# Two query tiles' scores in one TensorE visit, transpose mode for batch 0, and 128-row last stores that end on 16 outer steps

## The chip, the cores and the metric

The kernel runs on one core of a Trainium2 chip. The metric is the device time of one execution in microseconds, taken as the median of several runs. The engines are TensorE (PE; its weight loads are listed as PEld), VectorE (DVE), ScalarE (ACT), GpSimd (POOL) and SyncE (SP), which issues most DMAs.

## The reference

Eight batches of eight heads; 512 local and 32 global tokens per head, head size 64. A local query sees the 32 global keys and the local keys at most 32 places away; a global query sees all. The 4608 x 512 result goes through a layer with a Mish activation. The weights arrive as 64-bit floats.

```python
def _attn_ref(q_l, k_l, v_l, q_g, k_g, v_g):
    k_all = np.concatenate([k_g, k_l], axis=2)
    v_all = np.concatenate([v_g, v_l], axis=2)
    s_g = scale * np.matmul(q_g, k_all.transpose(0, 1, 3, 2))
    out_g = np.matmul(sm(s_g), v_all)                       # sm: softmax over the last axis
    s_ll = scale * np.matmul(q_l, k_l.transpose(0, 1, 3, 2))
    s_ll = np.where(np.abs(pos[:, None] - pos[None, :]) <= 32, s_ll, -1000000000.0)
    s_lg = scale * np.matmul(q_l, k_g.transpose(0, 1, 3, 2))
    a_l = sm(np.concatenate([s_lg, s_ll], axis=-1))
    out_l = np.matmul(a_l, np.concatenate([v_g, v_l], axis=2))
    return np.concatenate([out_g, out_l], axis=2)

def _moe_ref(x, w_in, w_out):                               # x: 4608 x 512, d_ff 2048
    h = x @ w_in
    g = h * np.tanh(np.log1p(np.exp(h)))                    # for h <= 20
    return g @ w_out
```

## The kernel before

Two heads share the 128 partitions, so a batch has four head pairs (`hp`). The 512 local queries of a pair are four tiles `t` of 128; a tile sees a window of 192 or 224 keys, global ones included (`WIN`: 192, 224, 224, 192). For each unit (batch, pair, tile) the work is a chain over the engines:

- `scores` (L611): two fp32 products on TensorE, one per head, each with K = 64 on its own half of the array's rows, into two buffers `s` of the PSUM ring "sc" (three buffers, shared with `g` and `gu` of the global queries);
- `row_max` (L620, VectorE) adds the mask and takes the row's extreme while it copies the scores to `P`; `expo` (L629, ScalarE) takes the exponential and the sums;
- `P` is split into two fp16 parts `ph` and turned by a transposing DMA into `pt` (`p_hi`, `p_lo`, `p_turn`); in batch 0 (`TURNED = 1`) TensorE turns `P` instead by products with the identity (`p_cross`, L667, into `PT`), and likewise the normalised result `x` (`x_cross`, L682, into `XT`);
- `pv` (L702): 12 small fp16 products of `pt` with the values, into `U`; then normalisation and a second turn into `xh` and `xl`, the layer's inputs.

Once per head pair the 32 global queries go through the same steps on a path of their own: `g_scores` (L740, fp32, two halves of 64 columns of the array), and `g_pv` (L794), whose result goes to `xg`.

The layer works on 17 blocks of 256 rows: 16 of local rows, the last (block 16) of all the global rows in `xg`. Each block has 8 steps: `m1_mm` (L838, fp16 products into `h`), `mish` (L881, ScalarE), `g_hi` and `g_lo` (VectorE mostly, into `G`), `m2_mm` (L906, into `o`). `store` scales `o` into `ob` and sends it out. Each product is made of three fp16 products (high by high, high by low, low by high).

At the start, the 64-bit weights are loaded on ScalarE's DMA queue, rebuilt as fp32 by VectorE (L418 to L427), measured by TensorE (`w_stat`, L439) and split into two fp16 parts (`w_split`, with `rest` on TensorE for the first layer, L483).

The order on each engine is not the order of the code. A planner (`Plan`) gets every piece of work with its engine, an assumed duration and what it reads and writes, and lists it: of the pieces that are ready, the one with the lowest number goes first on its engine. The numbers follow the order in which `slot(u)` adds the work for unit `u`. Engines then run their lists in that order, with semaphores between them. In the last store of block 16, ScalarE scales the first 128 rows and VectorE the second, and SP issues both transfers; their target is written as 4 batches x 32 rows x 512 floats.

Of the kernel before, what the change touches and what calls it, by code (L numbers as in the profile page):

```python
# [240 lines left out]
def attn_mish_kernel(ctx: ExitStack, tc: tile.TileContext, qt, kt, vm, vg, qg, w1, w2, consts_in, out, w64):  # L241
# [76 lines left out]
    def dma(kib):  # L318
        return kib * 2.81
# [282 lines left out]


    def scores(b, hp, t):
        q, k, s = ("q", b, hp), ("k", b, hp), [("s", b, hp, t, h) for h in range(2)]
        c0, w, m0 = WIN[t]

        def go():
            for h in range(2):
                r = slice(h * 64, h * 64 + 64)  # L610
                T.matmul(X[s[h]][:, :w], X[q][r, t * 128:(t + 1) * 128], X[k][r, c0:c0 + w], start=True, stop=True)  # L611
        pl.add(PE, 620, go, r=[q, k], new=[("sc", s[0]), ("sc", s[1])], rows=0.5)

    def half(P, h, w):
        return X[P][:, h * 224:h * 224 + w]

    def row_max(b, hp, t, h):
        s, P, nm = ("s", b, hp, t, h), ("P", b, hp, t), ("nm", b, hp, t, h)
        c0, w, m0 = WIN[t]
        pl.add(DVE, 155 + 1.04 * w, lambda: V.tensor_tensor_reduce(  # L620
            out=half(P, h, w), in0=X[s][:, :w], in1=mask[:, m0:m0 + w], scale=-SCALE, scalar=3.0e38, op0=ALU.add, op1=ALU.min,
            accum_out=X[nm]), r=[s, "consts"], w=[[P, h]] if h else (), new=[("nm", nm)] if h else [("P", P), ("nm", nm)])

    def expo(b, hp, t, h):
# [33 lines left out]
    def p_cross(b, hp, t):  # L658

        P, pt, PT = ("P", b, hp, t), ("pt", b, hp, t), ("PT", b, hp, t)  # L660
        rows = 128 if t else 96

        def go():
            for h in range(2):
                for c in range(2):
                    c0, n = h * 224 + c * rows, h * 2 + c
                    T.matmul(X[PT][:rows, n * 128:(n + 1) * 128], X[P][:, c0:c0 + rows], ident, start=True, stop=True)  # L667
        pl.add(PE, 1000, go, r=[P, "consts"], new=[("h", PT)], rows=0.5)

        def part(p):  # L670
            return X[pt][:rows, p * 4:p * 4 + 4, :].rearrange("p n q -> p (n q)")
        pl.add([(ACT, act(512)), (DVE, dve(512))], 0, lambda e: scaled(e, part(0), X[PT][:rows], PSC), r=[PT], new=[("pt", pt)])
        pl.add(DVE, dve(512), lambda: V.scalar_tensor_tensor(part(1), X[PT][:rows], PSC, part(0), ALU.mult, ALU.subtract), r=[PT], w=[pt])

    def x_cross(b, hp, t):
        g, ts = group(b, hp, t)
        x, XT, n, c0 = ("x", *g), ("XT", *g), 128 * len(ts), ts[0] * 128
        first = hp == 0 and ts[0] == 0

        def go():  # L680
            for i, u in enumerate(ts):
                T.matmul(X[XT][:, i * 128:(i + 1) * 128], X[x][:, u].rearrange("p h d -> p (h d)"), ident, start=True, stop=True)  # L682
        pl.add(PE, 250 * len(ts), go, r=[x, "consts"], new=[("h", XT)], rows=0.5)
        hi, lo = ("xh", b), ("xl", b)
        keys = [(hp, h) for h in range(2) if 2 * h in ts]
        cut = lambda name: X[name][:, hp, c0:c0 + n]
        pl.add([(ACT, act(n)), (DVE, dve(n))], 0, lambda e: copy(e, cut(hi), X[XT][:, :n]), r=[XT], w=[[hi, k] for k in keys],
               new=[("xh", hi)] if first else ())
        pl.add(DVE, dve(n), lambda: V.tensor_tensor(cut(lo), X[XT][:, :n], cut(hi), ALU.subtract), r=[XT] + [[hi, k] for k in keys],
               w=[[lo, k] for k in keys], new=[("xl", lo)] if first else ())  # L690
# [94 lines left out]
    def g_pv(b, hp):  # L785
# [11 lines left out]
        pl.add(PE, mm(18, 69), go, r=[pt, vf, va], new=[("sc", u)])  # L797
        for h in range(2):
            r = slice(64 * h, 64 * h + 64)
            pl.add([(ACT, 290), (DVE, 158)], 0, lambda e, r=r, h=h: scaled(e, xg[r, hp, b * SG:(b + 1) * SG], X[u][r, 32 * h:32 * h + 32],  # L800
                                                                          X["sv", b][r, 2:3]), r=[u, ("sv", b)], w=[["xg", (b, hp, h)]])


# [109 lines left out]
    def store(blk):  # L913
        ob = ("ob", blk)
        for t in range(2):
            o, c = ("o", blk, t), ("c", blk)
            engs = [(ACT, 690), (DVE, 668)] if blk < 2 * B else [((ACT, 690), (DVE, 668))[t]] * 2
            pl.add(engs, 0, lambda e, t=t, o=o: scaled(e, X[ob][:, t], X[o], X[c][:, 1:2]), r=[o, [c, 1]], w=[[ob, t]],
                   new=() if t else [("ob", ob)])
            if blk < 2 * B:  # L920
                r0 = (blk // 2) * S + SG + (blk % 2) * TB + t * 128
                pl.add(DMA, dma(256), lambda r0=r0, t=t: load(out[r0:r0 + 128, :], X[ob][:, t]), r=[[ob, t]])
            else:
                a = out[t * 4 * S:(t * 4 + 1) * S, :]
                pl.add(DMA, dma(256), lambda a=a, t=t: load(bass.AP(a.tensor, a.offset, [[S * DM, 4], [DM, SG], [1, DM]]), X[ob][:, t]),
                       r=[[ob, t]])


    NU = B * 16
# [21 lines left out]
    def slot(u):  # L951
# [14 lines left out]
        for x in m:  # L966
            if x[1] == 0:
                blk_start(x[0])
        if fu:
            scores(*fu)  # L970
        if fu:
            row_max(*fu, 0)
# [213 lines left out]
```

## Time and profile before

| | |
|---|---|
| median of 3 runs | 994.0 us (993.28 to 994.28) |
| the profiled execution | 989.48 us, of which the span from the first to the last instruction is 987.5 us |
| mean granted TensorE clock | 0.988 |
| busy: PE, PEld, DVE, ACT, POOL | 946.3, 633.0, 568.0, 583.1, 12.8 us |
| DMA | 113.73 MB in 214392 packets |

A line of the timeline gives a start, a duration, engine, source line, operation, output and inputs, shapes and a count of merged instructions; in square brackets stands how long the engine was idle before and what released it. `L12` is line 12 of the kernel. A matmul's recorded duration includes its way through the array, so neighbouring matmuls overlap in time; what one costs in a stream is the distance between starts.

### The profile page before, as it was taken

The numbers are of one execution on the slowest core, as the hardware profiler recorded it, in microseconds if no ns is written. First come the engines' busy times: TensorE is split into PE (matmuls) and PEld (weight loads), VectorE is DVE, ScalarE is ACT, GpSimd is POOL, SyncE is SP. The second block draws the span as 40 slices with busy tenths as digits, with TensorE's granted clock in tenths as the row PEclk, the third lists the DMA queues.
The fourth block names the chain that finished last, engine by engine and source line by source line (L and its number), as shares of the span: only waits on it lengthen the run. The fifth ranks groups of instructions, "written<-read, shape, count | busy, mean of one in ns | idle before, by whom it ended". The sixth has DMA issues, their size and how long they took to land.

```text
span 987.5 us, 20674 instructions
## 1 busy us (share of the span) xinstructions
PE 946.3 (96%) x8124; PEld 633.0 (64%) x8124; DVE 568.0 (58%) x1733; ACT 583.1 (59%) x1187; POOL 12.8 (1%) x25
## 2 busy tenths in 40 slices
PE   4789899999999999999999999999999999999995
PEld 2556677666675666666666666666666666666663
DVE  6879777747777665755465556665555542322221
ACT  2356876767676686768676777586676751211110
POOL 3000000000000000000000000000000000000000
PEclk9879999999999999999999999999999999999998
DMA  9875135766687975746383545654543430000000
GB/s 362 267 243 171 48 112 109 148 128 170 123 170 148 196 151 102 170 110 125 73 187 78 128 93 130 130 133 90 107 89 64 73 63 27 23 1 22 1 22 21
DMA packets 214392, 113.73 MB, mean 115 GB/s; under 512 B 181144, under 2 KB 194584, under 8 KB 213272
## 3 DMA queue, kind: packets, MB, share of 16 engines
q1 hardware_dynamic: 209688, 95.65, 44.2%
q10 hardware_dynamic: 4608, 16.78, 4.8%
q8 instruction: 63, 1.03, 0.4%
q14 instruction: 33, 0.27, 0.1%
HBM read 46.32 MB, written 8.91 MB: 56 GB/s over the span
## 4 chain that ended last, share of the span: by engine, by line
PE 81%; DMA 9%; DVE 5%; ACT 3%; SPq 2%; issue 1%; ACTq 0%; DVEq 0%
PE h L838 33%; PE o L906 32%; PE s L611 6%; PE U L702 4%; DMA vraw<-in_vm 4%; DMA pt<-ph 3%; PE g L740 2%; PE gu L794 2%; SPq L322 1%; PE rest L483 1%; DMA q<-in_qt 1%; DMA va<-vgf 1%; DVE vmx L512 1%; PE PT L667 1%; DVE W L489 0%
## 5 line engine op out<-in xcount | busy, mean ns | idle before, releaser
L906 PE MATMUL o<-W,G 128*128 128x512 f16 x1632 | 386.2, 379 | 0.0
L838 PE MATMUL h<-xh,W 128*128 128x256 f16 x2048 | 376.3, 273 | 2.2 <-ACT W L326 2.2
L838 PEld LDWEIGHTS <-W 128*128 128x128 f16 x3264 | 309.0, 98 | 73.4 <-issue 13.0
L838 PE MATMUL h<-xl,W 128*128 128x256 f16 x1024 | 278.9, 272 | 0.0
L906 PEld LDWEIGHTS <-G 128*128 128x128 f16 x1632 | 155.1, 98 | 156.0 <-issue 8.5
L881 ACT ACTIVATE e<-h,c 128x512 f32<-128x512 f32 (+1 forms) x137 | 93.4, 683 | 165.1 <-PE h L838 157.2
L335 DVE TENSOR_SCALAR G<-e,c 128x512 f16<-128x512 f32 (+1 forms) x134 | 64.7, 483 | 165.9 <-ACT e L881 164.2
L629 ACT ACTIVATE P<-P,nm 128x192 f32<-128x192 f32 (+1 forms) x256 | 117.8, 461 | 58.4 <-DVE nm L620 52.1
L620 DVE CUSTOM_DVE_ANT_0 P<-s,consts 128x192 f32<-128x192 f32 (+1 forms) x256 | 89.9, 369 | 56.7 <-PE s L611 54.7
L649 DVE SCALAR_TENSOR_TENSOR ph<-P,ph 128x384 f16<-128x384 f32 (+1 forms) x112 | 65.3, 586 | 71.6 <-ACT ph L333 71.1
L894 DVE SCALAR_TENSOR_TENSOR G<-e,c,G 128x512 f16<-128x512 f32 (+1 forms) x137 | 102.3, 746 | 3.8
L611 PE MATMUL s<-k,q 64*128 64x192 f32 (+1 forms) x512 | 84.2, 399 | 11.6 <-DMA q<-in_qt 11.1
L881 ACT ACT_TABLE_LOAD x62 | 79.5, 1283 | 1.4 <-DVE W L427 0.4
L702 PEld LDWEIGHTS <-pt 96*128 96x128 f16 (+1 forms) x1536 | 59.6, 98 | 27.9 <-issue 10.7
L629 ACT ACT_TABLE_LOAD x59 | 75.7, 1283 | 1.0
L333 ACT ACTIVATE ph<-P 128x384 f16<-128x384 f32 (+1 forms) x110 | 59.7, 546 | 18.8 <-DMA pt<-ph 16.5
L611 PEld LDWEIGHTS s<-k,q 64*128 64x128 f32 x512 | 41.3, 190 | 41.8 <-issue 30.2
L702 PE MATMUL U<-va,pt 128*128 128x64 f16 (+1 forms) x768 | 56.4, 193 | 5.6 <-DMA pt<-ph 3.0
L702 PE MATMUL U<-vc,pt 96*128 96x64 f16 x768 | 55.3, 193 | 0.0
L629 ACT ACTIVATION_READ_ACCUMULATOR P<-P,nm 128x1 f32 x256 | 47.9, 187 | 0.0
L333 ACT ACTIVATE ob<-o,c 128x512 f32<-128x512 f32 x33 | 22.6, 685 | 22.3 <-PE o L906 22.1
L333 ACT ACTIVATE xg<-gu,sv 64x32 f32<-64x32 f32 x63 | 17.7, 281 | 25.1 <-PE gu L794 24.1
(110 smaller groups left out, 706.3 us busy)
## 6 DMA issues: line engine op xcount, KB each, us to landing
k<-in_kt SPq DMA_DIRECT2D x32, 320.0 KB, 3.3
wraw<-in_w ACTq DMA_DIRECT2D x17, 512.0 KB, 5.5
out<-ob SPq DMA_DIRECT2D x34, 256.0 KB, 2.3
q<-in_qt SPq DMA_DIRECT2D x32, 256.0 KB, 2.9
vraw<-in_vm SPq DMA_DIRECT2D x8, 1024.0 KB, 6.3
W<-in_w ACTq DMA_DIRECT2D x15, 512.0 KB, 5.5
vc<-vf SPq DMA_DIRECT2D x32, 128.0 KB, 2.3
va<-vf SPq DMA_DIRECT2D x32, 96.0 KB, 2.7
```

Of the source, the lines that this page charges most:

```text
L333: A.activation(out=dst, in_=src, func=AF.Copy, scale=c)
L335: V.tensor_scalar(dst, src, c, None, ALU.mult)
L611: T.matmul(X[s[h]][:, :w], X[q][r, t * 128:(t + 1) * 128], X[k][r, c0:c0 + w], start=True, stop=True)
L620: pl.add(DVE, 155 + 1.04 * w, lambda: V.tensor_tensor_reduce(out=half(P, h, w), in0=X[s][:, :w], in1=mask[:, m0:m0 + w], scale=-SCALE, sca ...
L629: pl.add(ACT, 460, lambda: A.activation(out=half(P, h, w), in_=half(P, h, w), func=AF.Exp, bias=X[nm], scale=-1.0, accum_out=X[sums][:, t, ...
L649: pl.add(DVE, dve(n), lambda: V.scalar_tensor_tensor(p_part(X[ph], t, 1), p_src(X[P], t), PSC, p_part(X[ph], t, 0), ALU.mult, ALU.subtract ...
L702: T.matmul(X[u][:, t, h, :], X[pt][:k, p * 4 + h * 2 + c, :], X[vx][:k, t, vl, h * 64:(h + 1) * 64], start=(n == 0), stop=(n == 5))
L740: T.matmul(X[g][half * 64:half * 64 + 64, c0:c0 + n], X[q][:, hp, :], rhs, start=True, stop=True)
L838: T.matmul(X[h][:, f * TB:(f + 1) * TB], wh(i, wl)[:, off:off + 128], X[x][:, d, o:o + TB], start=(n == 0), stop=(n == 11))
L881: chain(blk, i, ACT, 705, lambda a, z: A.activation(out=X[e][:, a:z], in_=hv(blk, i)[:, a:z], func=AF.Mish, bias=0.0, scale=X[c][:, 0:1]), ...
L894: chain(blk, i, DVE, 668, lambda a, z: V.scalar_tensor_tensor(gp(1, blk, i)[:, a:z], X[e][:, a:z], X["c", blk][:, 2:3], gp(0, blk, i)[:, a ...
L906: T.matmul(X[o], gp(g, blk, i)[:, f, t * 128:(t + 1) * 128], wh(8 + i, wl)[:, f * 512:(f + 1) * 512], start=(i == 0 and n == 0), stop=(i = ...
```

## The change

Three things. First, `scores` is called for even tiles only and makes the products of tiles `t` and `t + 1`, four in a row; the two tiles of one head lie side by side in one PSUM buffer (`cols`: 192 + 224 or 224 + 192 of its 512 columns). `row_max` of each tile is still a piece of its own in its own unit's slot and reads its part of the buffer. The planner is told 1140 ns for the visit in place of 620 for each tile. Second, `p_cross` and `x_cross` use TensorE's transpose mode, with the same operands; the durations told to the planner stay. Third, the global rows stand in `xg` as row by batch instead of batch by row (each write of 32 columns now has a step of 8 floats), so that each half of the last block is 16 rows of all 8 batches; each half is scaled in two pieces of 256 columns, one on ScalarE and one on VectorE, and the second transfer is issued by ScalarE.

```diff
     def scores(b, hp, t):
-        q, k, s = ("q", b, hp), ("k", b, hp), [("s", b, hp, t, h) for h in range(2)]
-        c0, w, m0 = WIN[t]
+        q, k, s = ("q", b, hp), ("k", b, hp), [("s", b, hp, t // 2, h) for h in range(2)]
 
         def go():
-            for h in range(2):
-                r = slice(h * 64, h * 64 + 64)
-                T.matmul(X[s[h]][:, :w], X[q][r, t * 128:(t + 1) * 128], X[k][r, c0:c0 + w], start=True, stop=True)
-        pl.add(PE, 620, go, r=[q, k], new=[("sc", s[0]), ("sc", s[1])], rows=0.5)
+            for u in (t, t + 1):
+                c0, w, m0 = WIN[u]
+                for h in range(2):
+                    r = slice(h * 64, h * 64 + 64)
+                    T.matmul(X[s[h]][:, cols(u)], X[q][r, u * 128:(u + 1) * 128], X[k][r, c0:c0 + w], start=True, stop=True)
+        pl.add(PE, 1140, go, r=[q, k], new=[("sc", s[0]), ("sc", s[1])], rows=0.5)
+
+    def cols(t):
+
+        a = WIN[t - 1][1] if t % 2 else 0
+        return slice(a, a + WIN[t][1])
...
     def row_max(b, hp, t, h):
-        s, P, nm = ("s", b, hp, t, h), ("P", b, hp, t), ("nm", b, hp, t, h)
+        s, P, nm = ("s", b, hp, t // 2, h), ("P", b, hp, t), ("nm", b, hp, t, h)
...
-            out=half(P, h, w), in0=X[s][:, :w], in1=mask[:, m0:m0 + w], ...
+            out=half(P, h, w), in0=X[s][:, cols(t)], in1=mask[:, m0:m0 + w], ...
...
-                    T.matmul(X[PT][:rows, n * 128:(n + 1) * 128], X[P][:, c0:c0 + rows], ident, start=True, stop=True)
+                    T.transpose(X[PT][:rows, n * 128:(n + 1) * 128], X[P][:, c0:c0 + rows], ident)
...
-                T.matmul(X[XT][:, i * 128:(i + 1) * 128], X[x][:, u].rearrange("p h d -> p (h d)"), ident, start=True, stop=True)
+                T.transpose(X[XT][:, i * 128:(i + 1) * 128], X[x][:, u].rearrange("p h d -> p (h d)"), ident)
...
-            ... scaled(e, xg[r, hp, b * SG:(b + 1) * SG], X[u][r, 32 * h:32 * h + 32],
+            ... scaled(e, xg[r, hp].rearrange("p (n b) -> p n b", b=B)[:, :, b], X[u][r, 32 * h:32 * h + 32],
...
     def store(blk):
...
             else:
-                a = out[t * 4 * S:(t * 4 + 1) * S, :]
-                pl.add(DMA, dma(256), lambda a=a, t=t: load(bass.AP(a.tensor, a.offset, [[S * DM, 4], [DM, SG], [1, DM]]), X[ob][:, t]),
-                       r=[[ob, t]])
+                for n, e in enumerate((ACT, DVE)):
+                    cut = slice(n * 256, (n + 1) * 256)
+                    pl.add([(e, 430)] * 2, 0, lambda _, e=e, cut=cut, t=t, o=o: scaled(e, X[ob][:, t, cut], X[o][:, cut], X[c][:, 1:2]),
+                           r=[o, [c, 1]], w=[[ob, (t, n)]], new=() if t or n else [("ob", ob)])
+                a = out[t * 16:, :]
+                pl.add(DMA, dma(256), lambda a=a, t=t: (nc.sync, nc.scalar)[t].dma_start(
+                    bass.AP(a.tensor, a.offset, [[DM, 16], [S * DM, B], [1, DM]]), X[ob][:, t]), r=[[ob, (t, n)] for n in range(2)])
...
-        if fu:
+        if fu and fu[2] % 2 == 0:
             scores(*fu)
```

On TensorE, in batch 4, where pair 1 begins; names are tile, batch, pair and so on (`s_4_1_0_0`: batch 4, pair 1, tile 0, head 0). Before:

```order
L906 LDWEIGHTS G_21_5504
L906 MATMUL o_5_1_5497<-W_72,G_21_5504 128x512
L611 MATMUL s_4_1_0_0_5695<-k_4_1_4568,q_4_1_4587 128x192
L611 MATMUL s_4_1_0_1_5696<-k_4_1_4568,q_4_1_4587 128x192
L702 LDWEIGHTS pt_4_0_2_5578
L702 MATMUL U_4_0_5517<-va_4_0_4785,pt_4_0_2_5578 128x64
```

and now, at the same place (here `s_4_1_0_0` is pair 1, tiles 0 and 1, head 0):

```order
L912 LDWEIGHTS G_21_5439
L912 MATMUL o_5_1_5445<-W_72,G_21_5439 128x512
L612 MATMUL s_4_1_0_0_5625<-k_4_1_4517,q_4_1_4440 128x192
L612 MATMUL s_4_1_0_1_5626<-k_4_1_4517,q_4_1_4440 128x192
L612 MATMUL s_4_1_0_0_5625<-k_4_1_4517,q_4_1_4440 128x224
L612 MATMUL s_4_1_0_1_5626<-k_4_1_4517,q_4_1_4440 128x224
L708 LDWEIGHTS pt_4_0_2_5527
L708 MATMUL U_4_0_5461<-va_4_0_4851,pt_4_0_2_5527 128x64
```

The products of tile 1 stood 134 rows further down, and have moved up behind those of tile 0. VectorE at the same place (ISA is the row maximum), before:

```order
L620 ISA P2_76,nm_4_1_0_1_5762<-s_4_1_0_1_5696,consts_65 128x192
L620 ISA nm_4_1_0_1_5762 128x1
L712 TENSOR_TENSOR x_4_0_5766<-U_4_0_5517,rs_4_0_5659 128x512
L541 SCALAR_TENSOR_TENSOR vgf_5_5764<-vgraw_5_3337,sv_5_5731,vgf_5_5764 128x2x128
L721 TENSOR_TENSOR xs_4_0_5769<-x_4_0_5766,xs_4_0_5769 128x512
L620 ISA P0_74,nm_4_1_1_0_5806<-s_4_1_1_0_5794,consts_65 128x224
```

and now:

```order
L626 ISA P2_76,nm_4_1_0_1_5698<-s_4_1_0_1_5626,consts_65 128x192
L626 ISA nm_4_1_0_1_5698 128x1
L626 ISA P0_74,nm_4_1_1_0_5700<-s_4_1_0_0_5625,consts_65 128x224
L626 ISA nm_4_1_1_0_5700 128x1
L718 TENSOR_TENSOR x_4_0_5702<-U_4_0_5461,rs_4_0_5507 128x512
L626 ISA P0_74,nm_4_1_1_1_5725<-s_4_1_0_1_5626,consts_65 128x224
```

The row maxima of tile 1 follow those of tile 0 almost at once, and it is the last of them that frees the two buffers of the visit. At the end of the program, ScalarE before:

```order
L881 ACTIVATE e_16_5_12202<-h_16_5_12164,c_16_11374 128x512
L881 ACTIVATE e_16_6_12243<-h_16_6_12205,c_16_11374 128x512
L881 ACTIVATE e_16_7_12267<-h_16_7_12247,c_16_11374 128x256 x2
L333 ACTIVATE ob_16_12316<-o_16_0_12049,c_16_11374 128x512
L1182 UNCONDITIONAL_BRANCH
```

and now:

```order
L887 ACTIVATE e_16_6_12115<-h_16_6_12077,c_16_11246 128x512
L887 ACTIVATE e_16_7_12139<-h_16_7_12119,c_16_11246 128x256 x2
L333 ACTIVATE ob_16_12188<-o_16_0_11921,c_16_11246 128x256
L333 ACTIVATE ob_16_12188<-o_16_1_11941,c_16_11246 128x256
L934 DMA out_0<-ob_16_12188 16x8x512
L1191 UNCONDITIONAL_BRANCH
```

ScalarE now scales a half of both results and issues the second transfer behind them; SP's list ends with the first transfer, also as 16x8x512, where it had two of 4x32x512. On the engines the rest keeps its kind and count; where it stands shifts by a few rows, since the planner was told other durations.

More of the change, by code (lines that the diff above doesn't have):

```diff
@@ L617, in row_max @@
     def row_max(b, hp, t, h):
-        s, P, nm = ("s", b, hp, t, h), ("P", b, hp, t), ("nm", b, hp, t, h)
+        s, P, nm = ("s", b, hp, t // 2, h), ("P", b, hp, t), ("nm", b, hp, t, h)
         c0, w, m0 = WIN[t]
         pl.add(DVE, 155 + 1.04 * w, lambda: V.tensor_tensor_reduce(
-            out=half(P, h, w), in0=X[s][:, :w], in1=mask[:, m0:m0 + w], scale=-SCALE, scalar=3.0e38, op0=ALU.add, op1=ALU.min,
+            out=half(P, h, w), in0=X[s][:, cols(t)], in1=mask[:, m0:m0 + w], scale=-SCALE, scalar=3.0e38, op0=ALU.add, op1=ALU.min,
             accum_out=X[nm]), r=[s, "consts"], w=[[P, h]] if h else (), new=[("nm", nm)] if h else [("P", P), ("nm", nm)])
@@ L799, in g_pv @@
             r = slice(64 * h, 64 * h + 64)
-            pl.add([(ACT, 290), (DVE, 158)], 0, lambda e, r=r, h=h: scaled(e, xg[r, hp, b * SG:(b + 1) * SG], X[u][r, 32 * h:32 * h + 32],
+            pl.add([(ACT, 290), (DVE, 158)], 0, lambda e, r=r, h=h: scaled(e, xg[r, hp].rearrange("p (n b) -> p n b", b=B)[:, :, b], X[u][r, 32 * h:32 * h + 32],
                                                                           X["sv", b][r, 2:3]), r=[u, ("sv", b)], w=[["xg", (b, hp, h)]])
@@ L916, in store @@
             o, c = ("o", blk, t), ("c", blk)
-            engs = [(ACT, 690), (DVE, 668)] if blk < 2 * B else [((ACT, 690), (DVE, 668))[t]] * 2
-            pl.add(engs, 0, lambda e, t=t, o=o: scaled(e, X[ob][:, t], X[o], X[c][:, 1:2]), r=[o, [c, 1]], w=[[ob, t]],
-                   new=() if t else [("ob", ob)])
             if blk < 2 * B:
+                pl.add([(ACT, 690), (DVE, 668)], 0, lambda e, t=t, o=o: scaled(e, X[ob][:, t], X[o], X[c][:, 1:2]), r=[o, [c, 1]],
+                       w=[[ob, t]], new=() if t else [("ob", ob)])
                 r0 = (blk // 2) * S + SG + (blk % 2) * TB + t * 128
```

## The prediction

> **What bounds the kernel now.** I read the page first, then the busy time by stage, then TensorE's waits, and only then single visits in the timeline.
>
> ```profile
> span 987.5 us, 20674 instructions
> PE 946.3 (96%) x8124; PEld 633.0 (64%) x8124; DVE 568.0 (58%) x1733; ACT 583.1 (59%) x1187; POOL 12.8 (1%) x25
> ```
>
> TensorE (PE) is busy for 96% of the span, the other engines for under 60%. An average hides stages, so the span is cut where its character changes (columns: microseconds, busy time and instructions of each engine, granted clock, DMA share, GB/s):
>
> ```profile
> 0.00:70.00 70.00, 46.92 (x286) 29.29 (x287) 52.47 (x155) 26.55 (x71) 9.14 (x17) 0.88 0.88 305
> 70.00:113.00 43.00, 40.21 (x365) 28.21 (x364) 37.54 (x114) 32.54 (x63) 0.71 (x2) 1.00 0.36 111
> 113.00:830.00 717.00, 711.55 (x6474) 477.33 (x6473) 440.49 (x1402) 498.69 (x1017) 2.98 (x6) 1.00 0.57 119
> 830.00:978.40 148.40, 147.58 (x1006) 98.18 (x1004) 37.49 (x65) 25.37 (x37) 0.00 (x0) 1.00 0.03 11
> 978.40:987.50 9.10, 0.00 (x0) 0.00 (x0) 0.00 (x0) 0.00 (x0) 0.00 (x0) 0.65 0.19 58
> ```
>
> Up to 70 us TensorE idles for a third of the time and the DMA engines are 88% busy: weights arrive and are rebuilt. From 113 us to 978 us TensorE idles for 5.5 us of 717 and 0.8 us of 148, so there a microsecond of TensorE work is a microsecond of span. In the last 9.1 us no engine computes at all: only the last stores run. TensorE's own waits (total, times, longest):
>
> ```profile
> PE U L702 <- DMA pt<-ph: 3.0, 3, 1.4
> PE h L838 <- ACT W L326: 2.2, 1, 2.2
> ...
> PE gu L794 <- DMA gpt<-gph: 1.8, 1, 1.8
> ...
> PE s L611 <- DVE nm L620: 0.4, 2, 0.2
> ```
>
> The wait for W ends the stage at 113 us: the weights of the first layer are split on ScalarE (ACT), and TensorE stands until that is done, however early it gets there.
>
> **Part 1: scores of two tiles in one visit.** A visit is two K=64 products, one per head, in fp32; the trace has two records (passes) for each. Here is one visit with 192 columns between products of the first layer, then one with 224 between a second-layer product and a U:
>
> ```profile
> 601.09 0.27 PE L838 MATMUL h<-xh,W 128*128 128x256 f16 x1
> 601.29 0.59 PE L611 MATMUL s<-k,q 64*128 64x192 f32 x4
> 601.82 0.28 PE L838 MATMUL h<-xh,W 128*128 128x256 f16 x1
> ```
>
> ```profile
> 612.65 0.38 PE L906 MATMUL o<-W,G 128*128 128x512 f16 x1
> 612.96 0.65 PE L611 MATMUL s<-k,q 64*128 64x224 f32 x4
> 613.54 0.20 PE L702 MATMUL U<-va,pt 96*128 96x64 f16 x1
> ```
>
> From start to start, less the 0.11 us that the h before it takes in a stream (126.44 to 126.55 below) or the 0.22 us of the o (6.49 us for 30, at the tail below), the visits cost 601.82 - 601.09 - 0.11 = 0.62 us and 613.54 - 612.65 - 0.22 = 0.67 us; a pair of tiles 1.29 us. How much of it is streaming? The neighbouring line L740 has two fp32 products behind each other in one visit, two column halves side by side, as the scores have two row halves:
>
> ```profile
> 262.71 0.44 PE L740 MATMUL g<-k,qg 128*64 128x256 f32 x2
> 262.98 0.39 PE L740 MATMUL g<-k,qg 128*64 128x256 f32 x2
> 262.98 0.14 PEld L740 LDWEIGHTS g<-k,qg 128*64 128x64 f32 x2
> 263.19 0.24 PE L740 MATMUL g<-k,qg 128*64 128x16 f32 x4
> ```
>
> The second pass of 256 columns gives way to the next product after 0.21 us, or 0.83 ns a column, and that product's weights (PEld) are loaded at 262.98, under the pass. The first pass takes 0.27 us, since a first load lies bare. So a visit streams 2 x 192 x 0.83 ns = 0.32 us (224: 0.37) and pays 0.30 us for going in, the bare load and coming out. Two tiles in one visit pay that once: 0.62 + 0.37 = 0.99 us in place of 1.29, a gain of 0.30 us a pair. The worst case is that both passes of the second tile wait for their 128-column load, 0.11 us each (the pace of such a load in the transposes below): the gain is then 0.08 us. I take 0.30, as L740 is the nearest row: same type, same two side-by-side parts, one visit. The number of records of L611 by stage:
>
> ```profile
> 70.00:113.00 43.00, 2.49 (x16) 1.20 (x16) 1.00 0.36 111
> 113.00:830.00 717.00, 70.95 (x452) 34.30 (x452) 1.00 0.57 119
> ```
>
> 452 records are 113 visits, 56.5 pairs: 56.5 x 0.30 = **17.0 us** (worst 4.5). VectorE (DVE) and ScalarE get two tiles' work at once and otherwise the same work; over 113 to 830 us they are busy 61% and 70%, so the burst is covered, and so is a start of an even tile's row maxima that comes later by the second tile's 0.37 us. The planner's new order has 8 more table loads on ScalarE, 134 for 126:
>
> ```profile
> L881 ACT ACT_TABLE_LOAD x62 | 79.5, 1283 | 1.4 <-DVE W L427 0.4
> ```
>
> 8 x 1.28 = 10 us of the 218 us that ScalarE idles there: nothing, unless the h buffers wait for its mish.
>
> **Part 2: transpose mode in batch 0.** A visit of L667 is four products of 128 columns with the identity, eight records:
>
> ```profile
> 126.44 0.27 PE L838 MATMUL h<-xh,W 128*128 128x256 f16 x1
> 126.55 1.06 PE L667 MATMUL PT<-consts,P 128*128 128x128 f32 x8
> 127.45 0.27 PE L838 MATMUL h<-xh,W 128*128 128x256 f16 x1
> ```
>
> 127.45 - 126.55 = 0.90 us, 0.112 us a record, no gap on either side. In transpose mode I expect one pass each, still as long as the load of its weights: 0.112 us, so 0.45 us a visit are saved. The bounds: the load is short too and the gain 0.68, or entering and leaving the mode costs the 0.30 us of a score visit and the gain is 0.15; or nothing overlaps (a rival below). Records of L667 by stage, then those of L682 (its transposes of x):
>
> ```profile
> 70.00:113.00 43.00, 4.41 (x32) 3.88 (x32) 1.00 0.36 111
> 113.00:830.00 717.00, 5.39 (x40) 4.86 (x40) 1.00 0.57 119
> ```
>
> ```profile
> 113.00:830.00 717.00, 1.82 (x12) 1.81 (x12) 1.00 0.57 119
> ```
>
> Half of 40 + 12 records go: 26 x 0.112 = **2.9 us** after 113 us (bounds 0.4 and 4.4). Before 113 us, 16 records of L611 (0.6 us) and 32 of L667 (1.8 us) would gain 2.4 us since 70 us; I count nothing, because the cover there is the wait for W, whose end the weights set; if that cover were gone, 2.4 us come on top.
>
> **Part 3: the last stores.** The end, with a 256-column ScalarE row for the price of a half:
>
> ```profile
> 971.14 0.47 ACT L881 ACTIVATE e<-h,c 128x256 f32<-128x256 f32 x1 [2.08 <-PE h L838]
> 976.97 0.69 ACT L333 ACTIVATE ob<-o,c 128x512 f32<-128x512 f32 x1 [5.36 <-PE o L906]
> 977.62 0.75 DVE L335 TENSOR_SCALAR ob<-o,c 128x512 f32<-128x512 f32 x1 [5.09 <-PE o L906]
> 977.68 1.39 SPq L322 DMA_DIRECT2D out<-ob  x2
> ```
>
> ```profile
> 971.10 6.49 PE o L906 x30
> ```
>
> The DMA engines' busy tenths, first in 976 to 988 us, then in 897 to 903 us, where block 14's two stores run (same bytes, 40 slices each), and the landing times of the out stores:
>
> ```profile
> DMA  0000000000422101222222222222222210000000
> ```
>
> ```profile
> DMA  0000000003999920000004000018999500000000
> ```
>
> ```profile
> DMA to landing us min/median/max: 2.0/2.0/2.6
> ```
>
> The last two stores keep about a quarter of the 16 engines busy for 6 us (slices of 0.3 us, to about 986 us); an ordinary pair keeps nearly all of them busy, for under 1 us each. Both move 128 rows of 2 KB; what differs is the outermost step of the target, 4 against 128. The change makes it 16. The Trainium skill, DMA: Bandwidth & Descriptors, section "Why a DMA increments its semaphore by 16 and not by 1", has a DMA use the largest number of engines up to 16 that divides the outermost dimension of both sides: 4 before, 16 after; the quarter in the row agrees with the 4. The halves on two engines end at 977.62 + 0.47 = 978.1 us in place of 978.4; with 2.4 us to landing (between 2.0 and 2.6) the data lie at 980.5 in place of 986.0: **5.5 us** (best 5.9; worst 0.3, if still four engines work). The strided writes of xg are 64 short pieces off the chain: nothing. SP gives its second store to ScalarE's queue, behind which nothing is left.
>
> **Sum.** 17.0 + 2.9 + 5.5 = 25.4 us. The profiled execution took 989.5 us (span 987.5 and 2.0 around it), 0.5% under the median of 994.0; it would take 964.1, and the median becomes 968.6 us. The DMA waits (3.0 and 1.8 us) stay as they are: the order gives odd tiles' chains more room, but TensorE comes 2% sooner; bounds 4.8 us either way.
>
> **Rivals.**
> - *The second tile's loads stay bare.* For it: L740's halves are columns, the scores' are rows, so the row is a neighbour, not the thing. Part 1 gives 4.5: 994.0 - 12.9 = 981.1 us.
> - *The feeding becomes the bound.* TensorE gets ahead of the transposing DMAs, and the waits for pt and gpt double: 973.4 us. Against it: each odd tile's scores now come a unit earlier.
> - *Transposes that do not overlap.* If each takes a whole record's time instead of its place in a stream, four take 1.1 us: the last of the eight above starts at 126.55 + 7 x 0.112 = 127.33 and ends at 126.55 + 1.06 = 127.61, 0.28 us later. Part 2 turns into -0.2 a visit, -1.3 in all: 972.8 us. The Trainium skill, TensorE: Matmul & The Clock Gate, Part 4, "PE-mode transpose", speaks for this: it has about 275 ns for a transpose in one kernel, by which the sum is the same as with 1.1 us a visit; no run here shows it yet.
> - *The clock falls with transposes.* The row of 0 to 70 us has 0.88 granted where TensorE idles; if 113 to 160 us, the rest of batch 0's transposes, fell to that, 47 x 0.12 = 5.6 us: 974.2 us. The same section says that transposes don't count as busy for the clock. Against it: 0.45 us of them stand between long streams.
> - *Still four engines in the last stores:* 973.8 us.
> - *Slower.* The ring "sc" has three buffers; a visit now takes two for four row maxima, not two. If the row maxima of odd tiles come late, TensorE stands in the scores, with all h and o queued behind. It eats the whole gain when each of 64 visits waits 25.4 / 64 = 0.40 us: 994 us or more. Against it: that wait is 0.4 us in all today, and the 56.5 visits after 113 us would lie some 12 us apart.
> - *Better:* the DMA waits vanish: 963.8 us.
>
> **How the numbers follow.** Forecast 0.56, bare loads 0.14, feeding 0.08, transposes without overlap 0.06, four engines 0.05, better 0.05, clock 0.03, slower 0.03. The likeliest gives 968.6. The range runs from 961 (better, with part of the 2.4 us before 113) to 981.5 (bare loads). About 0.2% (2 us) is what a measurement can tell from no change: faster 0.95, same 0.02, slower 0.03.
>
> **What would show it.** L611 records come in groups of eight, about 0.99 us from one neighbour to the other; eight spread over 1.2 us mean bare loads. L667's successor has four records 0.45 us long. The DMA tenths at the end read 9, and the span ends about 3 us after the last ob. A row "PE s <- DVE nm" of many microseconds means the ring; more than 4.8 us of TensorE waiting for DMAs means the feeding.

## The result, and the profile after

The changed kernel takes 981.1 us (median; 979.7 to 985.7) against 993.6 us of the kernel before on the same chip: a ratio of 0.9903 (95% interval 0.9878 to 0.9928). The gain is 12.5 us; 25.4 were forecast. The profiled execution took 979.8 us, 9.7 us less than the profiled one of before. The page of after:

```profile
span 978.0 us, 20554 instructions
PE 922.8 (94%) x8044; PEld 629.6 (64%) x8044; DVE 572.9 (59%) x1750; ACT 573.6 (59%) x1180; POOL 13.6 (1%) x25
```

TensorE's busy time fell from 946.3 to 922.8 us. That is 23.5 us, and the forecast's work was 22.3 (17.0 + 2.9, and 2.4 before 113 us). But the span fell by only 9.5, so TensorE idles 14.0 us more. Where? The span is cut again by stage, at the end of the wait for W instead of at 113 us (stretch, its length, TensorE's busy time and instructions, granted clock, DMA share, GB/s). Before:

```profile
0.00:111.29 111.29, 85.42 (x632) 0.92 0.69 235
111.29:160.00 48.71, 48.31 (x413) 1.00 0.41 97
160.00:400.00 240.00, 236.80 (x2274) 1.00 0.71 147
400.00:830.00 430.00, 428.15 (x3808) 1.00 0.50 106
830.00:987.50 157.50, 147.58 (x1006) 0.98 0.04 14
```

and after:

```profile
0.00:116.24 116.24, 80.44 (x595) 0.88 0.69 228
116.24:160.00 43.76, 42.22 (x360) 0.96 0.43 93
160.00:400.00 240.00, 228.86 (x2224) 1.00 0.69 144
400.00:830.00 430.00, 428.35 (x3901) 1.00 0.50 108
830.00:978.00 148.00, 142.95 (x976) 0.99 0.04 15
```

Length less busy time is idle time. The change of the span, term by term, in us:

| term | before | after | difference | forecast |
|---|---|---|---|---|
| the wait for W ends at | 111.29 | 116.24 | +4.95 | 0 |
| busy from there on | 860.84 | 842.38 | -18.5 | -19.9 |
| idle from there to 830 us | 5.45 | 14.33 | +8.9 | 0 |
| idle from 830 us on (nearly all the last stores) | 9.92 | 5.05 | -4.9 | -5.5 |
| span | 987.5 | 978.0 | -9.5 | -25.4 |

The work and the stores came nearly as forecast. The 18.5 us of work hold two effects that nearly cancel: some 16 records (12 of h, 4 of scores, about 1.8 us) now lie ahead of the wait, and behind it the granted clock is at half for some 3 us (about 1.5 us more, see the last section). What was lost against the forecast is 4.95 us at the start and 8.9 us of waits, 7.9 of these between 160 and 400 us (11.14 for 3.20). TensorE's waits after, from 113 to 830 us (total, times, longest):

```profile
PE U L708 <- DMA pt<-ph: 4.8, 7, 1.6
PE h L844 <- ACT W L326: 4.5, 1, 4.5
PE gu L800 <- DMA gpt<-gph: 4.0, 4, 1.5
PE U L708 <- DVE x L718: 1.3, 1, 1.3
PE U L708 <- DVE pt L679: 1.3, 1, 1.3
PE U L708 <- DVE nm L626: 1.2, 1, 1.2
PE s L612 <- ACT xg L333: 0.8, 1, 0.8
```

Before, pt had 3.0 us there, gpt 1.8, and W 2.2 just ahead of 113 us. So 4.0 of the 8.9 us stand at the two transposing DMAs; most of the rest stands at pieces of VectorE and ScalarE. (U does not read nm, so what that wait was for is not known.) The last row is the PSUM ring of the "slower" rival: xg frees the buffer of gu, and TensorE stands in the middle of a visit, once, for 0.8 us. It did not happen at the size of that rival.

**The parts, one by one.** A visit of two tiles after, between an h and a U:

```profile
637.22 0.27 PE L844 MATMUL h<-xh,W 128*128 128x256 f16 x1
637.42 0.97 PE L612 MATMUL s<-k,q 64*128 64x224 f32 x8
638.33 0.26 PE L708 MATMUL U<-va,pt 96*128 96x64 f16 x3
```

638.33 - 637.22 - 0.11 for the h = 1.00 us; the forecast had 0.99, and 1.29 for the two visits that it replaces. The second tile's loads are hidden. A visit of transposes:

```profile
126.76 0.27 PE L844 MATMUL h<-xh,W 128*128 128x256 f16 x1
126.87 0.60 PE L673 MATMUL PT<-consts,P 128*128 128x128 f32 x4
127.30 1.46 PE L912 MATMUL o<-W,G 128*128 128x512 f16 x6
```

Four records in place of eight, 127.30 - 126.87 = 0.43 us (0.45 forecast, 0.90 before). The Trainium skill, TensorE: Matmul & The Clock Gate, Part 4, "PE-mode transpose", has about 275 ns for one in one kernel (its figures are for bf16), an estimate of 1.1 us for four. The trace does not agree with that sum: the four overlap, 0.11 us from one to the next, though one record by itself takes about as long (0.60 - 3 x 0.11 = 0.27 us). The end, engines and queues:

```profile
972.34 0.47 ACT L333 ACTIVATE ob<-o,c 128x256 f32<-128x256 f32 x1 [5.35 <-PE o L912]
972.85 0.48 DVE L335 TENSOR_SCALAR ob<-o,c 128x256 f32<-128x256 f32 x1 [4.95 <-ACT ob L333]
972.99 0.47 ACT L333 ACTIVATE ob<-o,c 128x256 f32<-128x256 f32 x1 [0.17 <-PE o L912]
973.36 0.64 SPq L934 DMA_DIRECT2D out<-ob  x1
973.50 0.48 DVE L335 TENSOR_SCALAR ob<-o,c 128x256 f32<-128x256 f32 x1 [0.17 <-ACT ob L333]
974.01 0.65 ACTq L934 DMA_DIRECT2D out<-ob  x1
```

The two column halves were meant to run side by side. They run one behind the other: VectorE starts when ScalarE's half is done (972.85 after 972.34 + 0.47, 973.50 after 972.99 + 0.47); what orders them was not tested. The busy tenths of the DMA engines and the landing times, 960 to 978 us (slices of 0.45 us):

```profile
DMA  0000000000001000000000000000000048995000
...
out<-ob SPq DMA_DIRECT2D x1, 256.0 KB, 3.0
out<-ob ACTq DMA_DIRECT2D x1, 256.0 KB, 3.0
```

The 9s say that nearly all engines work, for about 2 us in place of 6 us of 2s. With this the trace agrees with the Trainium skill's rule that the prediction cites (DMA: Bandwidth & Descriptors, section "Why a DMA increments its semaphore by 16 and not by 1"). From the issue at 974.01 the data need 3.0 us, not 2.4.

**The late W.** The last copy of a rest into W, what stands ahead of it on ScalarE, and the TensorE product that makes the rest. Before:

```profile
107.40 0.38 PE L484 MATMUL rest<-W,minus 128*128 128x512 f16 x1
...
110.58 0.19 ACT L453 ACTIVATE wp<-wp 128x1 f32<-128x1 f32 x1
110.67 0.57 ACT L326 CAST W<-rest 128x512 f16<-128x512 f32 x1
```

After (ScalarE, then TensorE: the product, and the first h behind the wait):

```profile
111.70 0.19 ACT L453 ACTIVATE wp<-wp 128x1 f32<-128x1 f32 x1
...
113.97 1.13 ACT L333 ACTIVATE W<-W,sw 128x1024 f16<-128x1024 f32 x1
115.01 0.71 ACT L333 ACTIVATE vf<-vraw,sv 128x512 f16<-128x512 f32 x1
115.62 0.56 ACT L326 CAST W<-rest 128x512 f16<-128x512 f32 x1
```

```profile
108.73 0.38 PE L484 MATMUL rest<-W,minus 128*128 128x512 f16 x1
...
116.24 0.37 PE L844 MATMUL h<-xh,W 128*128 128x256 f16 x1 [4.51 <-ACT W L326]
```

The rest is there at 109.1 us (107.8 before), and ScalarE copies it 6.5 us later (2.9 before). Of the 4.95 us, 3.6 are this longer way to the copy: the new order puts other pieces between wp and the copy, two exponentials, value rows, and a split of the next weights (113.97). No piece got slower; one piece changed its row. The other 1.3 us are the rest's own delay, which was not traced further. The moment also varies from one execution to the next: with the same list the wait ends at 117.80 us in e5 and at 114.00 in e4 below; with the list of before it ends at 111.08 and 111.15 in e2 and e3.

### The profile page after: what moved, and what is told of

It is laid out like the page before. It is cut to its first block, busy times and chain, and to the rows that moved or that the text cites. A ratio compares the mean times of both kernels' runs of the same rounds, so it can differ in the third digit from the quotient of the medians.

```text
span 978.0 us, 20554 instructions
## 1 busy us (share of the span) xinstructions
PE 922.8 (94%) x8044; PEld 629.6 (64%) x8044; DVE 572.9 (59%) x1750; ACT 573.6 (59%) x1180; POOL 13.6 (1%) x25
## 4 chain that ended last, share of the span: by engine, by line
PE 70%; DMA 12%; DVE 8%; ACT 6%; SPq 2%; issue 1%; ACTq 0%; POOL 0%; DVEq 0%
PE o L912 29%; PE h L844 29%; PE s L612 3%; PE U L708 3%; DMA vraw<-in_vm 3%; DMA pt<-ph 3%; DMA gpt<-gph 2%; PE g L746 1%; ACT P L635 1%; PE gu L800 1%; SPq L322 1%; DMA va<-vf 1%; DVE P L626 1%; DMA k<-in_kt 1%; SPq L500 1%
## 5 line engine op out<-in xcount | busy, mean ns | idle before, releaser
L626 DVE CUSTOM_DVE_ANT_0 P<-s,consts 128x192 f32<-128x192 f32 (+1 forms) x256 | 87.0, 368 | 15.5 <-PE s L612 14.2
L612 PE MATMUL s<-k,q 64*128 64x192 f32 (+1 forms) x512 | 67.4, 374 | 12.3 <-DMA q<-in_qt 11.2
L655 DVE SCALAR_TENSOR_TENSOR ph<-P,ph 128x448 f16<-128x448 f32 (+1 forms) x112 | 62.9, 587 | 22.7 <-ACT ph L333 21.0
L612 PEld LDWEIGHTS s<-k,q 64*128 64x128 f32 x512 | 44.9, 193 | 29.7 <-issue 19.8
L333 ACT ACTIVATE ph<-P 128x384 f16<-128x384 f32 (+1 forms) x106 | 53.9, 539 | 11.1 <-DMA pt<-ph 10.5
L333 ACT ACTIVATE ob<-o,c 128x512 f32<-128x512 f32 (+1 forms) x34 | 22.7, 668 | 23.3 <-PE o L912 23.2
```

The lines of the kernel that those rows point to most:

```text
L333: A.activation(out=dst, in_=src, func=AF.Copy, scale=c)
L612: T.matmul(X[s[h]][:, cols(u)], X[q][r, u * 128:(u + 1) * 128], X[k][r, c0:c0 + w], start=True, stop=True)
L626: pl.add(DVE, 155 + 1.04 * w, lambda: V.tensor_tensor_reduce(out=half(P, h, w), in0=X[s][:, cols(t)], in1=mask[:, m0:m0 + w], scale=-SCALE ...
L655: pl.add(DVE, dve(n), lambda: V.scalar_tensor_tensor(p_part(X[ph], t, 1), p_src(X[P], t), PSC, p_part(X[ph], t, 0), ALU.mult, ALU.subtract ...
```

## The experiments

Two theories of the lost time. *Order*: the planner was told other durations, so it wrote another list for every engine; the waits come from where single pieces stand in it. *Speed*: TensorE has got ahead of the DMAs and engines that feed it, and would wait in any list. Times are medians, ratios are to the kernel before on the same chip. "Idle" is TensorE's, up to 113 us, from there to 830, and from 830 on; busy and span are of the profiled execution:

| kernel | idle 0-113 | 113-830 | 830- | busy | span | time | ratio (95%) |
|---|---|---|---|---|---|---|---|
| before | 25.9 | 5.5 | 9.9 | 946.3 | 987.5 | 993.6 | 1 |
| changed | 32.6 | 17.6 | 5.1 | 922.8 | 978.0 | 981.1 | 0.9903 (0.9878-0.9928) |
| e1 scores only | 31.0 | 18.0 | 10.0 | 935.0 | 994.0 | 992.3 | 1.0004 (0.9983-1.0026) |
| e2 transposes only | 32.0 | 8.9 | 9.9 | 941.4 | 992.3 | 990.8 | 0.9990 (0.9974-1.0005) |
| e3 stores only | 29.9 | 5.4 | 5.1 | 945.1 | 985.5 | 986.8 | 0.9960 (0.9940-0.9981) |
| e4 changed + filler | 32.3 | 9.3 | 5.1 | 938.5 | 985.2 | 992.2 | 1.0001 (0.9986-1.0017) |
| e5 changed again | 33.3 | 19.9 | 5.0 | 924.3 | 982.5 | 984.2 | 0.9908 (0.9886-0.9931) |
| e6 changed, old costs told | 34.2 | 12.2 | 5.1 | 923.5 | 975.0 | 972.4 | 0.9804 (0.9780-0.9828) |
| e7 changed, global scores earlier | 34.6 | 15.4 | 5.0 | 922.8 | 977.9 | 979.9 | 0.9883 (0.9862-0.9904) |
| e8 true costs told, global scores earlier | 34.0 | 23.7 | 5.1 | 931.8 | 994.5 | 993.3 | 1.0012 (0.9993-1.0030) |
| e9 changed, pv later | 33.7 | 19.1 | 5.0 | 923.7 | 981.4 | 983.4 | 0.9914 (0.9885-0.9943) |
| e10 before, pv later | 28.6 | 9.7 | 9.9 | 946.6 | 994.8 | 996.3 | 1.0055 (1.0035-1.0075) |
| e11 changed, 1060 told | 32.4 | 22.8 | 5.1 | 925.2 | 985.5 | 985.4 | 0.9938 (0.9908-0.9967) |
| e12 e6 + e7 + e9 | 33.6 | 12.0 | 5.0 | 920.0 | 970.6 | 973.6 | 0.9826 (0.9790-0.9862) |
| e13 e6 + filler | 32.1 | 10.8 | 5.1 | 936.7 | 984.7 | 986.1 | 0.9937 (0.9915-0.9959) |
| e14 changed, last copy on VectorE | 34.6 | 26.6 | 5.0 | 924.1 | 990.2 | 995.3 | 1.0032 (1.0011-1.0053) |
| e15 before, 560 told | 25.7 | 16.3 | 10.0 | 950.7 | 1002.6 | 1002.3 | 1.0102 (1.0076-1.0128) |
| e16 before, 640 told | 30.1 | 12.7 | 9.9 | 947.5 | 1000.2 | 1001.0 | 1.0089 (1.0062-1.0116) |

A profiled execution can lie up to 5.2 us from its kernel's median (e4: 987.0 us for 992.2; e6: 976.8 for 972.4). The ratio decides on the time, the idle columns say where it went. The column 113-830 also holds what of the wait for W lies behind 113 us: 3.2 us in the changed kernel, 4.5 in e1 and e5, 1.0 in e4. And it scatters: the changed kernel has 17.6 and, in e5, 19.9; before has 5.5, and e2, with the same list, 8.9. Smaller differences are not read here.

**One part at a time.** e1 keeps the scores' part of the diff, e2 the two `T.transpose` lines, e3 the stores' part.

> The change's scores alone, with the order that the planner makes of them; transposes and last stores as before. In the profile of the changed kernel, TensorE's work after the wait for W is 19.5 us less than before, the last stores are 4.9 us shorter, the wait for W ends 4.9 us later and TensorE stands 9.6 us longer afterwards. Both theories hold that the scores' new order brings both losses: 17.0 us of work saved, less 4.9 and 9.6, so 2 to 3 us under the kernel before (about 991 us). If one of the losses comes from the transposes or the stores instead, this kernel is 5 to 10 us faster than that.

> The transpose mode alone: the planner is told nothing new, so the order is that of the kernel before. The changed kernel's trace has 0.55 us for a visit of L673 where it was 0.90; five visits and six single transposes after 113 us save 5 x 0.35 + 6 x 0.11 = 2.4 us if nothing else changes (about 991.2 us). If transposes lowered the clock or switched the array at a cost, nothing or a loss.

> The last stores alone, with the new place of the global rows. From the last o to the end of the span the changed kernel takes 5.0 us where it was 9.9: 4.9 us faster (about 988.7 us). If four engines' transfers were not the cause, 0.3 us.

(A visit of transposes costs 0.43 us, as above; the 0.55 us of the second expectation is too much by about one h, 0.11 us.)

The stores alone give 0.4%: their pieces stand last and move nothing else (113 to 830 us: 5.4 us of idle, as before). e1 lowers TensorE's busy time by 11.3 us (the records of the scores alone by 15.9, from 84.2 to 68.2; others took longer) and gains nothing: idle between 113 and 830 us rises by 12.5, to that of the whole change. e2 lowers it by 4.9 us and gains 0.1%, inside its interval. So the loss comes in with the scores, the part that changes most of TensorE's work and tells the planner another cost.

**The same order, a slower TensorE.** e4 adds two products of 176 columns to each visit; e13 adds the same to e6. No piece changes its row.

```diff
+            for h in range(2):
+                r = slice(h * 64, h * 64 + 64)
+                T.matmul(X[s[h]][:, cols(u)][:, :176], X[q][r, u * 128:(u + 1) * 128], X[k][r, c0:c0 + 176], start=True, stop=True)
```

> The changed kernel with two more products of 176 columns in each visit of the scores, which repeat a part of the last tile's products: 2 x 176 x 0.83 ns = 0.29 us a visit, 56.5 visits after 113 us, 16.4 us of TensorE work, in the same order on every engine. Theory 1 (order: the new waits come from where pieces stand in ScalarE's and VectorE's lists, for instance 20 more table loads ahead of the global queries' exponentials): the waits of about 15 us after the wait for W shrink by 3 us at most, 994 to 998 us. Theory 2 (speed: TensorE has got ahead of what feeds it): they fall back to the 5 us of the kernel before, about 988 us.

> The kernel with the planner's old costs (972.4 us, 0.9804) with two more products of 176 columns at the end of each visit of two tiles, as in the filler run before: the order on every engine stays, and TensorE gets back about 16 us of work. Speed theory (the later waits come because TensorE is ahead of the transposing DMAs, whatever the order): in the same order the later waits fall from 13.4 us to about 6, and the time rises by 9 to 10 us, to 0.990 of the kernel before. Order theory (the waits hang on the rows' places): the waits stay at 13 us and the time rises by 16 us, to 0.997.

In e4 busy time rises by 15.7 us, and idle from the end of the wait for W (114.00 us there) to 830 us falls from 14.3 to 8.3. With TensorE near its old pace 6.0 us of the waits are gone, which is speed; 8.3 against the 5.5 of before stay, which is order. These are single executions, and e4's is the fastest of twelve. The medians say the same within their scatter: 992.2 us lies between the two expectations (988, and 994 to 998), and the ratio rises by 0.0098, some 10 us, for 15.7 us of work. In e13 busy time rises by 13.2 us and the idle from 113 us falls from 12.2 to 10.8, less than the scatter; the ratio of 0.9937 lies halfway between the two expectations. Both theories hold a part, and how much depends on the list.

**The same work, another order.** e15 and e16 are the kernel before, with one number changed that only the planner reads.

```diff
-        pl.add(PE, 620, go, r=[q, k], new=[("sc", s[0]), ("sc", s[1])], rows=0.5)
+        pl.add(PE, 560, go, r=[q, k], new=[("sc", s[0]), ("sc", s[1])], rows=0.5)
```

> The kernel before, with the same instructions, and the planner told 560 ns for the scores of a tile in place of 620: only the order on the engines differs. Order theory: the time moves by 3 us or more, in either direction, through the end of the wait for W or through later waits of more than 9 us. Speed theory: TensorE is no faster than before, so the later waits stay under 8 us and the time within 0.3% of the kernel before (989 to 995 us).

> The same with 640 ns told. Order theory: 3 us or more in either direction. Speed theory: within 0.3% of the kernel before, later waits under 8 us. The last copy to W stands in ScalarE's list right behind the copy that it stood behind before, so the wait for W should end at 111 to 112 us in both theories.

They are 1.02% and 0.89% slower, and order theory's 3 us or more came out as 10 and 9. From 160 to 400 us, e15 and then e16:

```profile
160.00:400.00 240.00, 229.86 (x2166) 0.98 0.69 141
```

```profile
160.00:400.00 240.00, 229.98 (x2168) 0.99 0.69 140
```

10.1 and 10.0 us of idle with TensorE as slow as before, where before has 3.2 and the changed kernel 11.1. The waits of e15 from 113 to 830 us:

```profile
PE U L702 <- DMA pt<-ph: 6.8, 6, 3.6
PE gu L794 <- DMA gpt<-gph: 2.5, 3, 2.0
```

These are the same rows, led by the same transposing DMA. So a new list alone, with TensorE no faster, can make later waits of this size. What the prediction took as the kernel's own ("3.0 and 1.8 us") belonged mostly to one list, told 620: of the 18 profiles only before and e3 have less than 8 us of idle in 113 to 830, and e2 has 8.9, all three with that list up to the last stores.

**Other lists for the changed kernel.** e6 tells the planner what it was told before: 620 for the visit, and an empty piece of 620 where the odd tile's scores stood. e11 tells 1060.

```diff
-        pl.add(PE, 1140, go, r=[q, k], ...
+        pl.add(PE, 620, go, r=[q, k], ...
...
         if fu and fu[2] % 2 == 0:
             scores(*fu)
+        elif fu:
+            pl.add(PE, 620, lambda: None, r=[("q", *fu[:2]), ("k", *fu[:2])], rows=0.5)
```

> The changed kernel once more, beside the next three on one chip, since single runs lie up to 1% apart: ratio to the kernel before 0.988 to 0.992. In the trace, both theories: waits after the wait for W 12 to 17 us, the wait for W ending near 116 us.

> The changed kernel, but the planner is told what it was told before: 620 ns for an even tile's visit (with both tiles' products in it) and an empty piece of 620 ns for the odd tile. TensorE's work is that of the changed kernel. In the order, the last rest's copy to W stands ahead of the logarithm of wp again, as before the change, but 20 table loads still stand ahead of the global queries' exponentials. Order theory: the wait for W ends near 111 us, some 5 us of the changed kernel's loss, the waits for gpt stay: 5 us under the changed kernel. Speed theory: TensorE waits for W as long as before plus what it saves, and the later waits stay at 15 us: no gain after 116 us, and at most 1 to 2 us in all.

> The changed kernel with one number changed: the planner is told 1060 ns for the visit, not 1140. TensorE's work is the same. In the order the last rest's copy to W stands ahead of the logarithm of wp, not behind the split of the first weights of the second layer. If that place is the cause of the late wait for W, that wait ends at 111 to 113 us, not 116 to 118, and the kernel is 3 to 5 us under the changed one, give or take what the new order does later (waits of 10 to 18 us). If the wait for W were late because TensorE does its work sooner, it would end near 116 us here too.

e6 is the best of all, 0.9804 (0.9780 to 0.9828), 972.4 us: 20.0 us under the kernel before on that chip (992.3), 11.8 under the changed kernel run beside it (e5). Its list is not the old one: in it the last copy to W stands ahead of `wp` (before, right behind it), TensorE waits 0.4 us for the copy, and the idle from 113 to 830 is 12.2 us. In e11, too, the copy stands ahead of `wp`:

```profile
111.51 0.59 ACT L326 CAST W<-rest 128x512 f16<-128x512 f32 x1 [0.49 <-PE rest L484]
```

It follows its product at once, and the profile shows no wait of TensorE for it; the expectation's first case came true. But 2.6 us of waits for the next layer's weights follow by 120 us (2.8 in e6 by 121 us), the idle from 113 to 830 us is 22.8 us in all, and the kernel takes 985.4 us. So where the copy stands early the wait for W goes, and what that gives can be lost again in the rest of the same list.

**Taking single waits away.** e7 lets the global queries' scores and exponentials go one tile earlier in the later batches. After the change ScalarE reloads its table ahead of the global exponentials 23 times, where it did 3 times:

```profile
L768 ACT ACT_TABLE_LOAD x23 | 29.5, 1283 | 55.7 <-DVE gmx L763 55.7
```

```diff
-        if t == 2:
+        if t == (2 if b < HALVED else 1):
             g_scores(b, hp)
```

(and the same for the exponentials). e8 does this too and tells the planner costs nearer to the measured ones: 1000 for the visit, 546 for four transposes of P (0.43 us above) and 109 for each of x.

> The changed kernel with the global queries' scores, their exponentials and their turn added one unit earlier in batches 2 to 7, next to the visit of tiles 2 and 3. In the order, ScalarE's table loads fall from 134 to 106, those ahead of the global exponentials from 23 to 4; the copy to W stays late. TensorE's work is unchanged. Order theory: the waits for gpt go, and those for pt shrink with ScalarE 36 us less busy; of 15 us, 8 or fewer stay: 5 to 8 us under the changed kernel, about 974 to 976 on its scale of 981. Speed theory: the chains of DMAs that TensorE outruns are as long as before: 13 us or more of waits, within 2 us of the changed kernel.

> As the last one, and the planner is told what the trace measures for the change's visits: 1000 ns for two tiles' scores, 546 for four transposes, 109 for each transpose of x. In the order the copy to W stands right behind wp, as before the change, and table loads are 100. Order theory: the wait for W ends near 111 us, and 8 us or fewer of waits stay: 10 to 13 us under the changed kernel, about 969 us. Speed theory: within 3 us of the changed kernel.

In e7 the reloads fall to the old level:

```profile
L768 ACT ACT_TABLE_LOAD x4 | 5.1, 1283 | 0.3 <-DVE gmx L763 0.2
```

and the ratio falls from the 0.9908 of e5, run beside it, to 0.9883, some 2.5 us, with overlapping intervals. The waits of e7 from 113 to 830 us say why it is no more:

```profile
PE U L708 <- DMA pt<-ph: 7.8, 9, 1.9
...
PE gu L800 <- DMA gpt<-gph: 0.8, 1, 0.8
```

That is 3.2 us less for gpt than in the changed kernel and 3.0 more for pt (e5 has 5.3 and 5.6). Without the reloads most of the loss is still there; whether they caused the waits for gpt is open, as the list changed too. In e8 the idle from 113 to 830 us is 23.7 us, and its later waits are mostly of one kind. Its row of the waits, and the stretch in which they lie:

```profile
PE U L708 <- DMA pt<-ph: 20.2, 15, 3.6
```

```profile
160.00:400.00 240.00, 216.80 (x2035) 0.93 0.67 137
```

The granted clock there is 0.93 besides, the whole busy time is 9.0 us above the changed kernel's, and nothing is left of the gain, though the wait for W ends at 111.75 us as expected. The waits suggest that, planned by shorter costs, `pv` stands too near to the DMA that feeds it; this was not tested. A planner that was told truer costs wrote the worse list here.

e9 and e10 put `pv` (and the blocks that need it) one unit later from unit 32 on, in the changed kernel and in the one before; e12 is e6, e7 and e9 together. One line of e9's edit is shown; two more move the blocks and lengthen the loop by one unit.

```diff
-        fu, bu, vu = unit(u + 1), unit(u), unit(u - 1)
+        fu, bu, vu = unit(u + 1), unit(u), unit(u - 1) if u - 1 < 32 else unit(u - 2) if u - 2 >= 32 else None
```

> The changed kernel with pv and what follows it added one unit later in batches 2 to 7 (blocks 4 to 16 of the layer one unit later with it): more of TensorE's other work, some 6 us, lies between the turn of P and its use. No work is added. Speed theory (TensorE has got ahead of the DMAs that feed pv, and waits for too little slack): the waits after the wait for W fall from 15 or 16 us to 6 or fewer; about 9 us under the changed kernel, 973 to 975 on its scale of 982. Order theory (the waits come from where single pieces stand, which this shuffles anew): waits of 10 to 16 us stay, within 4 us of the changed kernel. The wait for W stays late, near 116 us, in both.

> The kernel before with the same extra unit. Its waits after the wait for W are 5.6 us. Speed theory: they fall to 3 or fewer, so 2 to 4 us faster than the kernel before, and the distance to the run before this one is then the work of the change: 19 us after the wait for W, 5 us of the stores, less what the wait for W ends later (5 us), about 19 us. Order theory: 0 to 10 us of waits, by chance.

> All of it together: the plan as told before the change (620 ns and an empty piece), the global queries' scores a unit earlier, and pv a unit later. Copy to W early, 6 table loads ahead of the global exponentials. Speed theory: the wait for W ends near 113 us, at most 6 us of waits follow: 994 - 19.4 (work) - 4.9 (stores) - 0 to 2 = 967 to 970 us, ratio 0.973 to 0.977. Order theory: 10 us or more of waits, no better than the run with the old plan alone (ratio 0.980).

More room for the DMAs did not help: e9's 983.4 us is the changed kernel's time, and its idle 19.1. That speaks against speed as the whole cause. e10 is 0.55% slower than before, where speed theory had it faster. e12 is no better than e6 alone.

**The one row.** e14 gives the last copy to W to VectorE alone.

```diff
-                pl.add([(ACT, act(512)), (DVE, dve(512))], 0, lambda e, rest=rest, cols=cols: copy(e, wh(j, 1)[:, cols], X[rest]),
+                pl.add([(DVE, dve(512))] * 2 if j == 7 else [(ACT, act(512)), (DVE, dve(512))], 0, lambda e, rest=rest, cols=cols: copy(...),
```

> The changed kernel; the last copy of the rest to W in the first layer's split is given to VectorE alone, so that it no longer stands behind eight pieces of ScalarE's list. If that row's place is what ends the wait for W 4.9 us later, the wait ends by 111 to 113 us and the time is 976 to 978 us (0.985), as long as the later waits don't grow. If the later waits take it back (TensorE is then 4 us further ahead of the DMAs), the time is 980 to 981 us (0.989). If something else holds W, the wait ends at 116 us and the time is 981.

No case came true. The wait for W still ended late, now through VectorE, where the copy also stands behind other pieces:

```profile
PE U L708 <- DMA pt<-ph: 14.9, 11, 4.2
...
PE h L844 <- DVE W L328: 4.2, 1, 4.2
```

and the list that follows from this one edit costs 14.9 us for pt, three times as much: 995.3 us. The experiment did not isolate the row: no single piece could be moved here without a new list for all. How much an earlier copy by itself would give back, in an otherwise unchanged list, stays untested.

## Why the prediction was wrong by half

Right: a pair's visit (1.00 us for 0.99), the visit of transposes (0.43 for 0.45), and that the stores take 16 engines. The busy time behind the wait for W fell by 18.5 us of 19.9 forecast. (The low bound of the second part comes out as 0.5 by its own rows, five visits at 0.15 and three pairs at 0.22 - 0.30, and not as 0.4; nothing rests on it.) Of the rivals, those on loads, transposes, engines and clock did not happen (the granted clock was 1.00 from 120 to 160 us, where transposes run), and the ring cost 0.8 us once. "Bare loads" gave 981.1 us, the measured median, but by another mechanism: the second tile's loads are hidden, so that the number fits is luck.

Wrong, in the order of size:

- *"The DMA waits (3.0 and 1.8 us) stay as they are ... bounds 4.8 us either way."* Idle from W to 830 us rose by 8.9 us. The rival on feeding, with a chance of 0.08, had the rows of pt and gpt and nearly their size (4.0 us more, 4.8 forecast), but not the other half of the 8.9, and it named speed as the only cause. e15 and e16 show that a new list suffices, with no speed gained; e4 shows that speed adds to it in the changed kernel's list (6.0 of 14.3 us go when TensorE is slowed), e13 that in another list it hardly does (1.4 of 12.2). The argument against the rival, that odd tiles' scores come earlier, did not hold the waits down.
- *"I count nothing, because the cover there is the wait for W, whose end the weights set."* The end was set by ScalarE's copy, 6.5 us behind the weights' product where it was 2.9, and a copy's row is the planner's choice. The end moved by 4.95 us, 3.6 of them by the copy's row.
- *The stores*: 4.9 us for 5.5. The landing took 3.0 us instead of 2.4, and the column halves, meant to run side by side, ran in sequence.
- *The table loads, "nothing, unless the h buffers wait for its mish"*: no such wait beyond 0.3 us showed, and e7, without the reloads of the global queries, is 2.5 us faster at most.

The other 2.8 us between the 9.7 of the two profiled executions and the 12.5 of the medians come from the choice of executions: before's lay 4.2 us under its median, after's 1.3 us under.

What stays open: which pieces of the new list make each wait between 160 and 400 us, and whether some list holds e6's work with the 5.5 us of idle of the old one. By e6's row that would be 972.4 - (12.2 - 5.5) = 966 us, an estimate near the forecast, from an execution 4.4 us above its median; no run reached it.

## What to carry to other kernels

Where a planner writes the order, a change of work is two changes: the work, which the profile prices well (here within 1.4 us of 19.9), and a new list, which can cost half of what the work gains (here 9 to 10 us from one number that no instruction reads). Before forecasting that the waits stay, run the old work under a slightly different list: waits of 5 us of 717, where each engine runs its list in order, belong mostly to that list, and the range of a forecast must hold another. When the work has changed, also run it with the old numbers told to the planner: here that gave 20.0 us in place of 12.5.

## What the runs showed of the hardware

Behind the wait of 2.2 us for W before the change the granted clock was 1.00 (111.29 to 160 us); behind that of 4.5 us after it, it was 0.50 at first. Stretches of TensorE around the wait for W after the change:

```profile
111.00:116.00 5.00, 0.73 (x7) 0.99 0.08 26
116.00:117.00 1.00, 0.76 (x4) 0.50 0.42 98
...
119.00:120.00 1.00, 1.00 (x5) 0.83 0.47 102
```

For some 3 us behind the wait the products start 0.21 us apart in place of 0.11, so the wait costs about 1.5 us more than its length, an estimate. The Trainium skill, TensorE: Matmul & The Clock Gate, Part 1, section "What's actually happening", has half rate after an idle window of about 3.4 us and full rate after as long a busy one; both waits agree with it.

In transpose mode an fp32 transpose of 128 x 128 leaves one record in the trace, 0.43 / 4 = 0.11 us in a stream, as long as one of the two records of the product with the identity (0.90 / 8).
